# Four fixed tiles per expert with seven further tiles between them, three weight buffers and a first group in two halves, in a fused sliding-attention and mixture-of-experts kernel

## The chip, the core and the metric

The kernel runs on one core of a Trainium2 chip. The metric is the device time of one execution in microseconds (us); lower is better. All arithmetic is float32.

## What is computed

Attention with a sliding window of 128 keys and a distance bias (8 batches, 8 heads, 576 positions, head size 64), then a mixture of experts over the 4608 resulting rows of 512 numbers: each row goes to the one expert of 8 with the largest gate logit.

```python
scores = where((rel >= 0) & (rel < 128), q @ k.T / sqrt(64) - slope[h] * abs(rel), -1e9)
attn   = softmax(scores) @ v                       # (8, 8, 576, 64)
x      = attn.transpose(0, 2, 1, 3).reshape(4608, 512)
logits = x @ w_gate                                # (4608, 8)
e      = logits.argmax(1)                          # one expert per row
y      = relu(x @ w1[e]) @ w2[e]                   # w1: 512 x 1024, w2: 1024 x 512
out    = softmax(logits)[e] * y
```

The inputs are drawn with a fixed seed. Worked out from the reference, the eight experts receive 547, 614, 590, 502, 618, 462, 608 and 667 rows.

## The kernel before

**Attention.** 32 units `u` (batch `b` = u // 4, pair of heads `hp` = u % 4) run one after the other on TensorE. Unit `u` computes `scores(u)`, DVE multiplies the exponentials with the bias factors (`factors`), GpSimd adds the two halves of each window in `merge(u)` (tile `mg`, lines 439 and 442), and one unit later TensorE runs `values(u - 1)` and `totals(u - 1)`; `totals` (line 477) reads `mg`. After each batch a list of tasks (10 or 12: gate logits, picking the expert, ranking the rows, building and sending the finished rows) is worked off, up to three tasks per unit; `slow = u < 6` keeps them back at the start. A task of the last kind, `send`, issues `scatter` (line 174), an indirect DMA from GpSimd that writes 128 finished rows into the buffer `x_rows` in DRAM, each at the place that its expert and its rank within the expert give it.

**Rows that are not there.** Each expert owns 4608 rows of `x_rows`. Before any scatter, `clear_rows` (line 112) writes a marked zero row into the first `CAP` rows of each expert, one expert per unit for `u` = 1 to 8, on SyncE's DMA queue, which also carries the loads of q, k and v. The first scatter waits for all of these clears.

**Experts.** A tile is 128 rows of one expert. `NJ = 5` tiles per expert are computed whatever the routing says (`CAP` = 640 rows), so 40 tiles in 8 groups; rows past 640 are covered by further tiles of one tile each, whose expert (`xe`) and first row (`xr`) `extras` works out on DVE. `XU = 2` such tiles are always computed, after the eighth expert, and masked if empty; a loop at the end would take any more. A group goes through `gather` (SyncE DMA of its rows into `xg`, two buffers; two DMAs for a group of more than two tiles), `ready` (its weights `w1` and `w2`, 2 MB each, into one of two weight buffers), `turn` (transposes `tp`, line 734, copied to `xgT` by DVE, line 735), `layer1` (lines 744 to 751: 64 weight blocks, tile `hps`, relu into `h_sb` on DVE and ACT in turn), `tokens` (`si`, the output row numbers, lines 726 and 727, from the gathered rows) and `layer2` (line 757, tile `zp`; ACT scales it into `zo`, line 762; GpSimd scatters it to the output, line 763). The matmuls of layer 1 stream 320 columns at a time for a group of five tiles and 128 for a single tile; those of layer 2 always stream 512. In the trace each float32 matmul shows as two records.

The order of the work is that of the loop:

```python
for g, after in zip(groups, groups[1:] + [None]):
    if after is not None:
        gather(after)
        ready(after)
    layer1(g)
    tokens(g)
    if after is not None:
        turn(after)
    layer2(g)
```

SyncE issues in this order; on the other engines a scheduler may move instructions past each other, so the order per engine is shown below where it matters.

Of the kernel before, what the change touches and what calls it, by code (L numbers as in the profile page):

```python
# [15 lines left out]
P = 128  # L16
# [5 lines left out]
def kernel(  # L22
# [30 lines left out]
    NJ = 5  # L53
    CAP = NJ * P
    NX = -(-(N - CAP) // P)
    XU = 2
    NC = E * NJ + NX
    LC = NJ * HALF
# [123 lines left out]
    w_pools = [ctx.enter_context(tc.tile_pool(name="weights0", bufs=1)), None]  # L182
    n_loads = [0]

    def load_weights(w1_src, w2_src):
        w_pool = w_pools[n_loads[0] % 2]
        n_loads[0] += 1
        w1 = w_pool.tile([P, DB, F], F32, name="w1")
        w2 = w_pool.tile([P, FB, Dm], F32, name="w2")
        nc.sync.dma_start(w1[:], w1_src.rearrange("(a p) f -> p a f", p=P))  # L190
        nc.sync.dma_start(w2[:], w2_src.rearrange("(a p) d -> p a d", p=P))
        return w1, w2
# [150 lines left out]
    with tc.tile_pool(name="tab", bufs=1) as tab, \  # L343
# [233 lines left out]
        with tc.manual_schedule():  # L577
# [10 lines left out]
            for u in range(NU + 1):  # L588
                b, hp = divmod(u, HP)

                slow = u < 6
# [19 lines left out]
                do(len(tasks) if u == NU else 0 if slow else 2)  # L611
# [96 lines left out]
    def moe_pools():  # L708
        st = ExitStack()
        pools["x"] = st.enter_context(tc.tile_pool(name="moe_x", bufs=2))  # L710
        pools["wk"] = st.enter_context(tc.tile_pool(name="moe_wk", bufs=2))
        w_pools[1] = st.enter_context(tc.tile_pool(name="weights1", bufs=1))
        pools["ps"] = st.enter_context(tc.tile_pool(name="moe_ps", bufs=3, space=PSUM))
        return st
# [14 lines left out]
    def turn(g):  # L729
        g["xT"] = pools["wk"].tile([P, DB, NJ * P], F32, name="xgT")  # L730
        for j in range(g["n"]):
# [5 lines left out]
    def layer1(g):  # L737
        g["h"] = pools["wk"].tile([P, FB, NJ * P], F32, name="h_sb")
        step = min(LC, g["n"] * P)
        for fb in range(FB):  # L740
            for c in range(0, g["n"] * P, step):
                hps = pools["ps"].tile([P, LC], F32, name="hps")
                for db in range(DB):
                    nc.tensor.matmul(  # L744
                        hps[:, :step], lhsT=g["w"][0][:, db, fb * P : (fb + 1) * P],
                        rhs=g["xT"][:, db, c : c + step], start=(db == 0), stop=(db == DB - 1),
                    )
                if fb % 2 == 0:
                    nc.vector.tensor_relu(g["h"][:, fb, c : c + step], hps[:, :step])  # L749
                else:  # L750
                    nc.scalar.activation(g["h"][:, fb, c : c + step], hps[:, :step], AF.Relu)  # L751
# [26 lines left out]
    def ready(g):  # L778
        if "x" in g:
            g["w"] = fetch(g["x"])  # L780
# [4 lines left out]
    def experts(first):  # L785
        groups = [
            dict(n=NJ, e=e, rows=x_d[e * N : e * N + CAP, :], mask=masks[:, :, e, :], apart=True)
            for e in range(E)
        ]
        gather(groups[0])  # L790
        ready(groups[0])
        turn(groups[0])
        extras(first)
        for x in range(XU):
            ex = nc.sync.value_load(xe[0:1, x : x + 1], min_val=0, max_val=E - 1)
            r0 = nc.sync.value_load(xr[0:1, x : x + 1], min_val=0, max_val=E * N - P)
            groups.append(
                dict(n=1, x=ex, rows=x_d[bass.ds(r0, P), :], mask=xmasks[:, :, x : x + 1], apart=True)
            )
        for g, after in zip(groups, groups[1:] + [None]):  # L800
            if after is not None:
                gather(after)
                ready(after)
            layer1(g)
            tokens(g)
            if after is not None:
                turn(after)
            layer2(g)
# [5 lines left out]
    with tc.If(more > 0):  # L814
# [10 lines left out]
        with tc.If(nx > XU):  # L825
            with moe_pools(), tc.For_i(XU, nx, 1) as i:
# [6 lines left out]
                turn(g)  # L833
                layer1(g)
# [31 lines left out]
```

## Time and profile before

| | |
|---|---|
| median of 3 runs (lowest, highest) | 857.45 us (854.78, 859.46) |
| the profiled execution | 855.47 us, its span 853.7 us |
| TensorE busy | 802.2 us, 94% of the span |
| DVE, ACT, GpSimd busy | 227.8, 173.9, 171.5 us |
| DMA moved | 112.56 MB, mean 132 GB/s |
| mean granted TensorE clock | 0.971 of full speed |

The span runs from the first to the last instruction; the time contains it and 1.8 us around it. "Idle before" in a row is the time for which the engine stood still ahead of that work, and after the arrow stands what ended it. A weight load (PEld) runs beside the matmuls (PE). The attention part lies in the first 240 us, the experts in the rest.

### The profile page before, as it was taken

The page shows a single profiled execution, that of the slowest core. Times are in us where ns is not written, and L with a number is a line of the kernel's source. Part 1 is how long each engine was busy: PE and PEld are TensorE (multiplying, and loading weights), DVE is VectorE, ACT ScalarE, POOL GpSimd, SP SyncE. Part 2 cuts the span into 40 slices and gives each one's busy share as a digit, 9 for nine tenths or more (in the row PEclk, how much of TensorE's full clock was granted, in tenths as well). Part 3 has the DMA queues.
Part 4 walks back from the last instruction along what each step waited for, and adds up shares of the span by engine and source line. Part 5 has one row for each costly group of instructions (what it writes and reads, how often), then busy time and mean ns, then how long its engine had stood idle before and what let it go on. Part 6 is the DMA issues. An engine that isn't in the chain of part 4 may idle for free.

```text
span 853.7 us, 10090 instructions
## 1 busy us (share of the span) xinstructions
PE 802.2 (94%) x4162; PEld 511.6 (60%) x4162; DVE 227.8 (27%) x475; ACT 173.9 (20%) x410; POOL 171.5 (20%) x189
## 2 busy tenths in 40 slices
PE   4997999999679999999999999999999999999993
PEld 3775777766557547646645754764664575475481
DVE  5463777887841101101200110110120011010010
ACT  3553556545200101001001010100100110010010
POOL 5344665656500010010010001001001000100100
PEclk8898999999779999999999999999999999999997
DMA  9994895531244016017004201600701420150060
GB/s 347 342 355 191 317 336 172 193 108 52 100 160 173 19 47 246 5 45 268 1 37 164 116 25 50 232 13 37 269 0 38 171 96 25 54 190 12 37 225 5
DMA packets 47335, 112.56 MB, mean 132 GB/s; under 512 B 3503, under 2 KB 3503, under 8 KB 47280
## 3 DMA queue, kind: packets, MB, share of 16 engines
q1 hardware_dynamic: 40512, 92.89, 30.8%
q0 software_dynamic: 6240, 18.92, 5.9%
q8 instruction: 35, 0.57, 0.3%
q14 instruction: 20, 0.16, 0.1%
q10 hardware_dynamic: 528, 0.02, 0.0%
HBM read 82.37 MB, written 31.01 MB: 133 GB/s over the span
## 4 chain that ended last, share of the span: by engine, by line
issue 69%; PE 15%; POOL 9%; DVE 5%; ACT 1%; POOLq 0%; DVEq 0%
PE sp L413 5%; POOL out_dram L763 5%; PE m L458 4%; PE sm L477 2%; PE m L556 2%; POOL x_rows L174 1%; POOL mg L439 1%; DVE probs L427 1%; PE m L498 1%; POOL mg L442 1%; DVE probs L432 1%; ACT gex L536 1%; DVE lgn L532 1%; PE m L514 1%; DVE xs L559 0%
## 5 line engine op out<-in xcount | busy, mean ns | idle before, releaser
L757 PE MATMUL zp<-w,h_sb 128*128 128x512 f32 x672 | 292.4, 592 | 0.0
L744 PE MATMUL hps<-xgT,w 128*128 128x320 f32 (+1 forms) x1152 | 291.8, 415 | 0.0
L744 PEld LDWEIGHTS hps<-xgT,w 128*128 128x128 f32 x1152 | 209.0, 190 | 83.9 <-issue 4.3
L757 PEld LDWEIGHTS zp<-w,h_sb 128*128 128x128 f32 x672 | 125.8, 190 | 149.2 <-issue 149.2
L749 DVE TENSOR_SCALAR h_sb<-hps 128x320 f32<-128x320 f32 (+1 forms) x72 | 33.8, 469 | 460.6 <-PE hps L744 460.6
L763 POOL DMA_INDIRECT out_dram<-zo,si x42 | 40.8, 971 | 567.1 <-ACT zo L762 567.1
L751 ACT ACTIVATE h_sb<-hps 128x320 f32<-128x320 f32 (+1 forms) x72 | 30.2, 419 | 277.1 <-PE hps L744 277.1
L762 ACT ACTIVATE zo<-zp,xg 128x512 f32<-128x512 f32 x42 | 28.9, 687 | 279.0 <-PE zp L757 279.0
L413 PE MATMUL sp<-q_sb,k_sb 64*128 64x256 f32 (+2 forms) x640 | 71.5, 368 | 6.4 <-DMA k_sb<-in_kT_dram 6.4
L420 ACT ACTIVATE e<-sp 128x512 f32<-128x512 f32 x128 | 66.2, 599 | 48.1 <-PE sp L413 44.8
L413 PEld LDWEIGHTS sp<-q_sb,k_sb 64*128 64x128 f32 x640 | 63.0, 199 | 17.8 <-issue 11.1
L439 POOL TENSOR_TENSOR mg<-probs 128x768 f32<-128x768 f32 x31 | 57.5, 1856 | 77.8 <-DVE probs L432 29.0
L458 PE MATMUL m<-probs,v_sb 128*64 128x256 f32 (+3 forms) x768 | 64.2, 316 | 3.7 <-DVE probs L427 2.8
L458 PEld LDWEIGHTS m<-probs,v_sb 128*64 128x64 f32 x768 | 48.4, 138 | 19.9 <-DVE probs L427 2.9
L427 DVE TENSOR_TENSOR probs<-e,fac 128x1024 f32<-128x1024 f32 x32 | 43.6, 1361 | 43.8 <-ACT e L420 34.1
L174 POOL DMA_INDIRECT x_rows<-xs,slots x36 | 39.8, 1104 | 22.8 <-issue 12.0
L432 DVE TENSOR_TENSOR probs<-e,fac 128x1024 f32<-128x1024 f32 x32 | 41.9, 1309 | 0.7 <-ACT e L420 0.5
L735 DVE COPY xgT<-tp 128x512 f32<-128x512 f32 x42 | 27.7, 688 | 45.2 <-PE tp L734 45.0
L477 PE MATMUL sm<-mg,one_c 128*32 128x320 f32 (+1 forms) x256 | 24.5, 373 | 11.0 <-POOL mg L442 11.0
L734 PE MATMUL tp<-ident,xg 128*128 128x128 f32 x168 | 24.6, 289 | 10.6 <-DMA xg<-x_rows 10.5
L734 PEld LDWEIGHTS tp<-ident,xg 128*128 128x128 f32 x168 | 21.3, 150 | 20.8 <-issue 13.9
L465 ACT COPY xT<-m 128x256 f32<-128x256 f32 x64 | 25.3, 402 | 22.9 <-PE m L458 22.9
(127 smaller groups left out, 282.3 us busy)
## 6 DMA issues: line engine op xcount, KB each, us to landing
w<-in_moe_w_dram SPq DMA_DIRECT2D x20, 2048.0 KB, 11.6
x_rows<-zero_row SPq DMA_DIRECT2D x8, 1285.0 KB, 16.8
v_sb<-in_v_dram SPq DMA_DIRECT2D x8, 1024.0 KB, 7.8
q_sb<-in_qT_dram SPq DMA_DIRECT2D x7, 1152.0 KB, 7.8
k_sb<-in_kT_dram SPq DMA_DIRECT2D x7, 1152.0 KB, 11.5
xg<-x_rows SPq DMA_DIRECT2D x8, 771.0 KB, 6.0
xg<-x_rows SPq DMA_DIRECT2D x8, 514.0 KB, 3.8
v_sb<-in_v_dram SPq DMA_DIRECT2D x8, 256.0 KB, 8.1
```

What stands on the lines that cost most here:

```text
L174: ins = nc.gpsimd.indirect_dma_start(out=x_d[:, :], out_offset=bass.IndirectOffsetOnAxis(ap=slots[:, t : t + 1], axis=0), in_=row, in_offs ...
L413: nc.tensor.matmul(sps[s][par][:, c : c + n], lhsT=k_sb[b][half, hp, k_lo[j] : k_lo[j] + P], rhs=q_sb[b][half, hp, q0 : q0 + n], start=Tru ...
L420: nc.scalar.activation(exps[u][s][:, par, :], sps[s][par][:], AF.Exp, scale=D ** -0.5)
L427: nc.vector.tensor_tensor(to.rearrange("p a (j c) -> p a j c", c=2 * P), e.rearrange("p a (j c) -> p a j c", c=2 * P), fac[:, heads, None, ...
L432: nc.vector.tensor_tensor(to, e[:], fac2[:, heads, :], op=ALU.mult)
L439: eng.tensor_add(mg[:, :, : 3 * P].rearrange("p a (t c) -> p a t c", c=P), two[:, :, :, 0, :], two[:, :, :, 1, :],)
L458: nc.tensor.matmul(xp[par * HALF : (par + 1) * HALF, lo - q0 : hi - q0], lhsT=v_sb[b][:, j, h * D : (h + 1) * D], rhs=probs[u][:, par, c + ...
L477: nc.tensor.matmul(sm[g : g + 32, c : c + n], lhsT=one_c[:, hp, :], rhs=src[:, par, s0 : s0 + n], start=(hp == 0 and c == 0), stop=(hp == ...
L734: nc.tensor.transpose(tp[:, db, :], g["xg"][:, j, db * P : (db + 1) * P], ident[:])
L744: nc.tensor.matmul(hps[:, :step], lhsT=g["w"][0][:, db, fb * P : (fb + 1) * P], rhs=g["xT"][:, db, c : c + step], start=(db == 0), stop=(d ...
L757: nc.tensor.matmul(zp[:], lhsT=g["h"][:, fb, j * P : (j + 1) * P], rhs=g["w"][1][:, fb, :], start=(fb == 0), stop=(fb == FB - 1),)
L763: ins = nc.gpsimd.indirect_dma_start(out=out[:, :], out_offset=bass.IndirectOffsetOnAxis(ap=g["si"][:, j : j + 1], axis=0), in_=zo[:], in_ ...
```

## The change

It sets `NJ = 4` (so `CAP` = 512 and 32 fixed tiles) and `XU = E - 1` = 7, and puts one further tile between every two experts: 15 groups in the order 4, 1, 4, 1, ..., 4. Layer 1 now streams a whole group at once (512 columns). There are three weight buffers, and a group's weights are asked for two groups ahead. The first group goes through `turn` and `layer1` in two parts of two tiles. In attention the tasks start at u = 7 and three instead of two are taken at the end of a unit while 14 or more wait.

```diff
-    NJ = 5
+    NJ = 4
...
-    XU = 2
-    NC = E * NJ + NX
-    LC = NJ * HALF
+    XU = E - 1
+    LC = NJ * P
...
-    w_pools = [ctx.enter_context(tc.tile_pool(name="weights0", bufs=1)), None]
+    w_pools = [ctx.enter_context(tc.tile_pool(name="weights0", bufs=1)), None, None]
...
-        w_pool = w_pools[n_loads[0] % 2]
+        w_pool = w_pools[n_loads[0] % len(w_pools)]
...
-                slow = u < 6
+                slow = u < 7
...
-                do(len(tasks) if u == NU else 0 if slow else 2)
+                do(len(tasks) if u == NU else 0 if slow else 2 if len(tasks) < 14 else 3)
...
-        w_pools[1] = st.enter_context(tc.tile_pool(name="weights1", bufs=1))
+        for i in range(1, len(w_pools)):
+            w_pools[i] = st.enter_context(tc.tile_pool(name=f"weights{i}", bufs=1))
...
-    def layer1(g):
-        g["h"] = pools["wk"].tile([P, FB, NJ * P], F32, name="h_sb")
-        step = min(LC, g["n"] * P)
+    def layer1(g, tiles):
+        if tiles[0] == 0:
+            g["h"] = pools["wk"].tile([P, FB, NJ * P], F32, name="h_sb")
+        cols = slice(tiles[0] * P, (tiles[-1] + 1) * P)
+        n = len(tiles) * P
...
         if "x" in g:
-            g["w"] = fetch(g["x"])
+            x = g["x"]
+            ex = nc.sync.value_load(xe[0:1, x : x + 1], min_val=0, max_val=E - 1)
+            r0 = nc.sync.value_load(xr[0:1, x : x + 1], min_val=0, max_val=E * N - P)
+            g["rows"] = x_d[bass.ds(r0, P), :]
+            g["w"] = fetch(ex)
...
+        groups = []
+        for e in range(E):
+            groups.append(dict(n=NJ, e=e, rows=x_d[e * N : e * N + CAP, :], mask=masks[:, :, e, :], apart=True))
+            if e < XU:
+                groups.append(dict(n=1, x=e, mask=xmasks[:, :, e : e + 1], apart=True))
         gather(groups[0])
         ready(groups[0])
-        turn(groups[0])
         extras(first)
...
+        parts = [[0, 1], list(range(2, NJ))]
+        turn(groups[0], parts[0])
+        layer1(groups[0], parts[0])
+        turn(groups[0], parts[1])
+        layer1(groups[0], parts[1])
+        ready(groups[1])
+        for i, g in enumerate(groups):
+            after = groups[i + 1 : i + 3]
+            if after:
+                gather(after[0])
+            if len(after) > 1:
+                ready(after[1])
+            if i > 0:
+                layer1(g, range(g["n"]))
             tokens(g)
-            if after is not None:
-                turn(after)
+            if after:
+                turn(after[0], range(after[0]["n"]))
             layer2(g)
```

**Place 1: GpSimd in attention, around the first scatter** (`mg` is the sum of `merge`, two rows per unit; `x_rows` is the scatter). Before:

```order
L442 TENSOR_TENSOR mg<-probs 128x2x64
L550 COPY xs<-tok_i 128x2
L439 TENSOR_TENSOR mg<-probs 128x2x384
L442 TENSOR_TENSOR mg<-probs 128x2x64
L174 DMA x_rows<-xs,slots 36864x514
L550 COPY xs<-tok_i 128x2
L174 DMA x_rows<-xs,slots 36864x514 x3
L439 TENSOR_TENSOR mg<-probs 128x2x384
L442 TENSOR_TENSOR mg<-probs 128x2x64
L439 TENSOR_TENSOR mg<-probs 128x2x384
```

Now:

```order
L438 TENSOR_TENSOR mg<-probs 128x2x384
L441 TENSOR_TENSOR mg<-probs 128x2x64
L549 COPY xs<-tok_i 128x2
L173 DMA x_rows<-xs,slots 36864x514
L549 COPY xs<-tok_i 128x2
L438 TENSOR_TENSOR mg<-probs 128x2x384
L441 TENSOR_TENSOR mg<-probs 128x2x64
L173 DMA x_rows<-xs,slots 36864x514 x3
L438 TENSOR_TENSOR mg<-probs 128x2x384
L441 TENSOR_TENSOR mg<-probs 128x2x64
```

The merge of unit 9 stood behind all four scatters of the first batch; now it stands behind the first alone, and the other three follow it.

**Place 2: SyncE's queue where the experts begin** (`xg` is a gather, `w` are weights; 2838 and 2839 are the second expert's `w1` and `w2`, 2911 and 2912 those of the first further tile, 2917 and 2918 the second expert's). Before:

```order
L721 DMA xg<-x_rows 128x2x514
L721 DMA xg<-x_rows 128x3x514
L795 TENSOR_LOAD xe
L795 ISA x2
L796 TENSOR_LOAD xr
L796 ISA x2
L795 TENSOR_LOAD xe
L795 ISA x2
L796 TENSOR_LOAD xr
L796 ISA x2
L721 DMA xg<-x_rows 128x2x514
L721 DMA xg<-x_rows 128x3x514
L190 DMA w_2838<-in_moe_w_dram 128x4x1024
L191 DMA w_2839<-in_moe_w_dram 128x8x512
```

Now:

```order
L721 DMA xg<-x_rows 128x2x514 x2
L783 TENSOR_LOAD xe
L783 ISA x2
L784 TENSOR_LOAD xr
L784 ISA x2
L189 ISA
L189 DMA w_2911<-in_moe_w_dram 128x4x1024
L190 ISA
L190 DMA w_2912<-in_moe_w_dram 128x8x512
L721 ISA
L721 DMA xg<-x_rows 128x514
L189 DMA w_2917<-in_moe_w_dram 128x4x1024
```

The second gather stood ahead of the weights; now that of the first further tile stands behind 4 MB of them. From the next group on, each gather again comes ahead of the weights that are asked for with it.

**Place 3: TensorE where the experts begin** (`tp` are transposes, four per tile; `hps` is layer 1, `zp` layer 2). Before:

```order
L734 MATMUL tp<-ident,xg 128x128 x20
L744 MATMUL hps<-xgT,w_1285 128x320
L691 MATMUL tp<-n_in,ones_sq 128x1
L744 MATMUL hps<-xgT,w_1285 128x320 x63
L734 MATMUL tp<-ident,xg 128x128 x8
L757 MATMUL zp<-w_1286,h_sb 128x512
```

Now:

```order
L690 MATMUL tp<-n_in,ones_sq 128x1
L735 MATMUL tp<-ident,xg 128x128 x12
L746 MATMUL hps<-xgT,w_1285 128x256 x32
L735 MATMUL tp<-ident,xg 128x128 x8
L759 MATMUL zp<-w_1286,h_sb 128x512
L746 MATMUL hps<-xgT,w_1285 128x256 x32
L759 MATMUL zp<-w_1286,h_sb 128x512 x31
L746 MATMUL hps<-xgT,w_2911 128x128 x32
L735 MATMUL tp<-ident,xg 128x128 x8
L759 MATMUL zp<-w_2912,h_sb 128x512
```

Three tiles are now transposed ahead of the first half of layer 1; the eight transposes behind it are the fourth tile and the first further tile, which thus stands ahead of the second half. The small `n_in` matmul, on which `xe` depends, moved ahead of the transposes.

## Rows read from the trace of the kernel before

**Rows 1.** The page: busy us of each engine, share of the span, instructions.
```profile
PE 802.2 (94%) x4162; PEld 511.6 (60%) x4162; DVE 227.8 (27%) x475; ACT 173.9 (20%) x410; POOL 171.5 (20%) x189
```

**Rows 2.** Windows: busy us per engine (instructions), granted clock, DMA share, GB/s.
```profile
45.00:70.00 25.00, 24.24 (x284) 19.09 (x280) 16.71 (x33) 14.61 (x39) 7.94 (x8) 1.00 1.05 362
...
78.00:84.00 6.00, 5.22 (x26) 3.54 (x28) 2.56 (x10) 0.69 (x5) 3.01 (x5) 0.50 0.00 0
...
240.50:245.20 4.70, 4.57 (x21) 3.86 (x22) 2.96 (x6) 0.00 (x0) 0.00 (x0) 0.53 0.28 109
...
318.60:333.50 14.90, 14.90 (x57) 10.55 (x56) 2.30 (x6) 1.31 (x3) 0.00 (x0) 1.00 1.00 373
...
461.00:790.00 329.00, 329.00 (x1066) 194.75 (x1064) 34.82 (x71) 31.91 (x61) 20.41 (x21) 1.00 0.26 96
```

**Rows 3.** Timeline, SyncE: start us, us, DMA issues of two successive five-tile groups.
```profile
388.31 0.88 SPq L721 DMA_DIRECT2D xg<-x_rows  x2
...
459.29 0.88 SPq L721 DMA_DIRECT2D xg<-x_rows  x2
```

**Rows 4.** Timeline, TensorE: the first of the two single tiles.
```profile
811.46 7.31 PE L744 MATMUL hps<-xgT,w 128*128 128x128 f32 x64
818.60 0.60 PE L734 MATMUL tp<-ident,xg 128*128 128x128 f32 x4
819.04 7.03 PE L757 MATMUL zp<-w,h_sb 128*128 128x512 f32 x16
825.91 0.27 PE L744 MATMUL hps<-xgT,w 128*128 128x128 f32 x1
```

**Rows 5.** Timeline, TensorE, where the experts begin; then the last scaling and scatter.
```profile
240.56 4.76 PE L734 MATMUL tp<-ident,xg 128*128 128x128 f32 x20 [10.51 <-DMA xg<-x_rows]
245.16 0.70 PE L744 MATMUL hps<-xgT,w 128*128 128x320 f32 x2
...
840.12 0.69 ACT L762 ACTIVATE zo<-zp,xg 128x512 f32<-128x512 f32 x1 [6.59 <-PE zp L757]
841.08 0.97 POOL L763 DMA_INDIRECT out_dram<-zo,si  x1 [13.04 <-ACT zo L762]
```

**Rows 6.** Timeline of attention, TensorE and GpSimd around 70 us; who waited for the clears.
```profile
72.02 0.41 PE L477 MATMUL sm<-probs,one_c 128*32 128x128 f32 x4
78.78 1.28 PE L477 MATMUL sm<-mg,one_c 128*32 128x320 f32 x8 [6.34 <-POOL mg L442]
...
84.97 0.66 PE L556 MATMUL m<-ident,xT 128*128 128x128 f32 x4
...
70.68 1.45 POOL L174 DMA_INDIRECT x_rows<-xs,slots  x1 [7.09 <-issue]
...
76.50 1.82 POOL L439 TENSOR_TENSOR mg<-probs 128x768 f32<-128x768 f32 x1
...
  POOL x_rows L174: 7.1, 1
```

**Rows 7.** The page, DMA issues: count, KB each, us from issue to landing.
```profile
w<-in_moe_w_dram SPq DMA_DIRECT2D x20, 2048.0 KB, 11.6
x_rows<-zero_row SPq DMA_DIRECT2D x8, 1285.0 KB, 16.8
...
xg<-x_rows SPq DMA_DIRECT2D x8, 771.0 KB, 6.0
xg<-x_rows SPq DMA_DIRECT2D x8, 514.0 KB, 3.8
```

**Rows 8.** Timeline around a single tile's gather: ACT, SyncE, DVE; then `xe` at the start.
```profile
811.71 0.69 ACT L762 ACTIVATE zo<-zp,xg 128x512 f32<-128x512 f32 x1 [6.18 <-PE zp L757]
812.42 0.35 SPq L721 DMA_DIRECT2D xg<-x_rows  x1
815.57 0.16 DVE L726 TENSOR_TENSOR si<-xg,xmasks 128x1 int32<-128x1 int32 x1 [0.94 <-DMA xg<-x_rows]
...
236.70 13.75 SPq L721 DMA_DIRECT2D xg<-x_rows  x4
...
246.38 0.17 DVE L703 CAST xe<-xe_f 1x34 int32<-1x34 f32 x1
```

More of the change, by code (lines that the diff above doesn't have):

```diff
@@ L727, in tokens, with turn @@
         nc.vector.tensor_tensor(g["si"][:, :n], g["si"][:, :n], g["mask"][:, 1, :], op=ALU.bitwise_or)
-    def turn(g):
-        g["xT"] = pools["wk"].tile([P, DB, NJ * P], F32, name="xgT")
-        for j in range(g["n"]):
+    def turn(g, tiles):
+        if tiles[0] == 0:
+            g["xT"] = pools["wk"].tile([P, DB, NJ * P], F32, name="xgT")
+        for j in tiles:
             tp = pools["ps"].tile([P, DB, P], F32, name="tp", bufs=2)
@@ L735, in turn @@
             nc.vector.tensor_copy(g["xT"][:, :, j * P : (j + 1) * P], tp[:])
-    def layer1(g):
-        g["h"] = pools["wk"].tile([P, FB, NJ * P], F32, name="h_sb")
-        step = min(LC, g["n"] * P)
-        for fb in range(FB):
[L741 to L751, printed above, removed]
+    def layer1(g, tiles):
+        if tiles[0] == 0:
+            g["h"] = pools["wk"].tile([P, FB, NJ * P], F32, name="h_sb")
+        cols = slice(tiles[0] * P, (tiles[-1] + 1) * P)
+        n = len(tiles) * P
+        for fb in range(FB):
+            hps = pools["ps"].tile([P, LC], F32, name="hps")
+            for db in range(DB):
+                nc.tensor.matmul(
+                    hps[:, :n], lhsT=g["w"][0][:, db, fb * P : (fb + 1) * P], rhs=g["xT"][:, db, cols],
+                    start=(db == 0), stop=(db == DB - 1),
+                )
+            if fb % 2 == 0:
+                nc.vector.tensor_relu(g["h"][:, fb, cols], hps[:, :n])
+            else:
+                nc.scalar.activation(g["h"][:, fb, cols], hps[:, :n], AF.Relu)
     def layer2(g):
@@ L785, in experts @@
     def experts(first):
[L786 to L789, printed above, removed]
+        groups = []
[3 more added lines that the diff above has]
+                groups.append(dict(n=1, x=e, mask=xmasks[:, :, e : e + 1], apart=True))
         gather(groups[0])
         ready(groups[0])
-        turn(groups[0])
         extras(first)
[L794 to L800, printed above, removed]
-            if after is not None:
-                gather(after)
-                ready(after)
-            layer1(g)
+        parts = [[0, 1], list(range(2, NJ))]
[12 more added lines that the diff above has]
+                layer1(g, range(g["n"]))
             tokens(g)
-            if after is not None:
-                turn(after)
+            if after:
+                turn(after[0], range(after[0]["n"]))
             layer2(g)
@@ L832 @@
                 gather(g)
-                turn(g)
-                layer1(g)
+                turn(g, range(1))
+                layer1(g, range(1))
                 tokens(g)
```

## The prediction

> **What bounds the kernel now.** The page first: TensorE is busy for 802.2 of 853.7 us [rows 1]. Since a busy TensorE need not be one at full speed, the windows come next. In the experts' part it has no gap: 329.00 busy us in a stretch of 329 at full clock, with the DMA engines busy for 0.26 of it [rows 2]. There the time is the number of matmul columns, and a tile left out is a tile saved. The timeline then gives the price of a group. SyncE issues the gathers of successive five-tile groups at 388.31 and 459.29, so one group takes 70.98 us [rows 3]. The single tile at the end takes from 811.46 to 825.91, 14.45 us: 7.14 layer 1, 0.44 transposes, 6.87 layer 2 [rows 4]. Eight groups and two single tiles make 8 x 70.98 + 2 x 14.45 = 596.7 us. From the first transpose at 240.56 to the last matmul, whose result ACT takes up at 840.12, are 599.5 [rows 5]; the 2.8 above the sum lie at the start, where the granted clock is at 0.53 of full speed, the lower of its two levels (1.2 GHz), until layer 1 begins at 245.16 [rows 2, 5].
>
> Last, the gaps of TensorE before 240 us. The one that the change touches is at 72 us: `totals` waits 6.34 us for GpSimd's `mg` [rows 6]. GpSimd itself stood for 7.09 us at the first scatter, and the clears were what it waited for (the last row of rows 6). After this gap TensorE runs at the lower clock: 0.50 from 78 to 84 [rows 2].
>
> **The change, term by term.**
>
> *Tiles.* A group of four has 64 records of 512 columns in layer 1 and 64 in layer 2. Layer 2 of one tile is 16 such records in 6.87 us, 0.429 each [rows 4]; so 128 x 0.429 = 55.0, and four transposes of a tile at 0.44 add 1.8: 56.7. Pro rata from the five-tile group it is 0.8 x 70.98 = 56.8, so the two ways agree. A single tile is priced by the trace at 14.45. New sum: 8 x 56.7 + 7 x 14.45 = 554.8 against 596.7. **This term is -42.0 us.** Three tiles fewer (39 for 42) carry it; five more single tiles give back 5 x (7.14 - 6.87) = 1.4 of it, since a layer 1 of 128 columns costs 0.27 more per tile than columns alone.
>
> The narrow matmuls lose only those 0.27 us, 4% [rows 4]. The Trainium skill ("TensorE: Matmul & The Clock Gate", section "Back-to-back issue gap") gives a stream of load and matmul pairs about 81 ns per matmul at 128 columns and 131 at 512, so a column costs 2.5 times as much when narrow. An estimate by that ratio makes layer 1 of a single tile 17 us and the seven of them 69 us dearer, for a total of 875. The trace disagrees, for float32.
>
> *Fifteen weight loads for ten.* Each is 4.2 MB. The DMA engines move 373 GB/s when kept busy [rows 2], so a load is 11.3 us of transfer and fifteen are 169, beside 555 us of matmuls. A pair of groups (71.2 us) needs two loads and five tiles of rows, 26 us. Asked for two groups ahead, each load has a whole pair of groups to land. Cost 0; the cover is the four-tile group of 56.7 us.
>
> *Gathers behind single tiles.* A four-tile gather is issued when ACT has scaled the last tile of the group before, and must land during the single tile's layer 1. In the trace that order of events is: scaling at 811.71, gather issued at 812.42, layer 1 over at 818.60 [rows 8, 4]. The new gather is two pieces of 514 KB; a piece of that size lands 3.8 us after issue, and the second piece of a five-tile gather, larger, 6.0 [rows 7]. The second issue comes 0.44 us after the first (0.88 for two, [rows 3]), so: first piece at 816.2, second at 818.9 at the latest. The first transposes need the first piece alone; those of the other two tiles come 1.7 us later. Cost 0, upper end 7 x 0.3 = 2. Behind the waiting `si` on DVE [rows 8] stands one relu of the single tile, which layer 2 needs only for its seventh block.
>
> *Start of the experts.* Before, all five tiles were transposed in the slow 4.6 us. Now three tiles and the first matmuls fall into the same slow stretch, so its loss stays about 2.8 less 0.3. What is new is the single tile's transpose ahead of the second half of layer 1 (place 3). Its gather stands behind 4.2 MB of weights on SyncE (place 2). SyncE got the value `xe` only after 246.38 before, because the `n_in` matmul stood behind layer 1; now that matmul is first, so `xe` should be there by about 239, when DVE has done the routing arithmetic, and the weights go out near 241. 4.5 MB at 373 GB/s are 12 us, and a small gather has about 2.4 us of latency (3.15 from issue to use, [rows 8], less 0.7 of transfer): it lands near 255.8. The first half of layer 1 is 64 records at half of 0.429, 13.7 us, from about 243.3: it ends near 257. So the wait is 0 if `xe` is early, and up to 6 us, with 2.4 for a lowered clock, if `xe` is as late as before. I take **+1.0**, near the early end, because the order of the instructions speaks for it.
>
> The Trainium skill ("DMA: Bandwidth & Descriptors", section "HWDGE ordering") says that each DMA engine takes the descriptors of a ring in order, so the gather cannot overtake those weights. No row of this trace has a gather behind weights; without the rule the term would be 0 for certain.
>
> *Attention.* The clears shrink from five to four tiles per expert, 257 KB for each of eight, 2.1 MB in all. In that stretch the DMA engines are full at 362 GB/s (share 1.05, [rows 2]), so the last clear lands about 5.8 us earlier: the first scatter starts at 64.9 instead of 70.68. The merge that TensorE waited for now stands behind one scatter, not four (place 1): 64.9 + 1.5 for the scatter + 0.7 + 2.3 for the merge is 69.4, and `totals` wants it at 72.4. The gap of 6.34 goes, and with it the slow clock: the work from 78.78 to 84.97 is 6.2 us [rows 6] at half speed for most, of which I count 2.4 as lost. **-8.7**. The lower end is 0, if the clears land as late as before; the point is 67.9, above which the merge is late. Moving the tasks by one unit changes no TensorE work. What is late next is nothing long: the other gaps before 240 are in the first 22 us and in the wait for the last scatters, 10.51 [rows 5], which stays.
>
> *Relu, scaling, clearing of other engines*: DVE is busy for 35 of 329 us [rows 2]; nothing there becomes a bound. The tail after the last matmul is the same.
>
> **Sum.** 855.5 - 42.0 - 8.7 + 1.0 = **806 us**, against the profiled execution, which is 2.0 below the median of 857.45; the median of the new runs may lie as much above the sum.
>
> **Rivals.**
> - *The attention gap stays.* For it: the landing of the last clear is worked out from a mean rate, and the clear shares the queue with the load of the next batch. Against: the new order spares the merge three scatters in any case. Up to 8.7 comes back: 814.5. Chance 0.15.
> - *Single tiles are too short to hide the next gather.* For it: 818.9 against 818.60 has no room. Against: those seven places have no other transfer in the queue, as the weights asked for earlier have had 56 us. With 1.5 us at each of seven places, +10: 816. Chance 0.12.
> - *Slower than before: the gathers wait behind weights at all seven places.* Then each four-tile gather lands 11.3 us later, TensorE stands some 11 us and loses 2.4 more to the clock, 7 x 13.7 = 96: 902. From 7.2 us per place on it eats the 50 gained. Against: the order puts each gather ahead of the weights asked for with it (place 2). Chance 0.03.
> - *Narrow weights bind.* If each weight load of a single tile cost its full 0.19 us, layer 1 would be 64 x 0.19 = 12.2 and seven of them 35 dearer: 841. The trace has 7.14 [rows 4]. The skill's figures above point this way. Chance 0.01.
> - *The change does not do what it says*: an eighth further tile sends the kernel into the loop at its end, one unhidden load (11.3) and a tile (14.45) and its gather and branch, some 30 us: 836. The reference's counts need 1+1+1+0+1+0+1+2 = 7, and none lies within 9 rows of a boundary of 128. Chance 0.02.
> - *More is gained*: the early DMA relief removes other waits in the first 70 us. 799. Chance 0.07.
>
> **How the numbers follow.** The forecast of 806 has 0.60. The range takes in the first two rivals and the 2 us between profile and median, upward to 818, and downward the lighter clears, to 799. Left out are the slower, the narrow and the loop cases and part of the last. A measurement of this kernel can tell about 0.5%, 4.3 us, from no change. Faster by more than that: all cases but the slower one and some slack, 0.95; within: 0.02; slower: 0.03.
>
> **What would show each step.** Tiles: a fixed group and a single tile together take 71.2 us from gather to gather, without gaps of TensorE. Start: no wait of TensorE between the halves of layer 1 of more than 2 us. Attention: no gap near 72 us, first scatter near 65, first expert transpose near 232. Wrong would be: gaps of TensorE after each single tile, a clock below full in the experts' part, or a first scatter that still starts at 70.

## The result, and the profile after

| | before | the change |
|---|---|---|
| median of 4 runs each (lowest, highest) | 856.12 us (854.57, 859.46) | 809.07 us (806.76, 809.21) |
| the profiled execution, its span | 855.47, 853.7 us | 808.99, 807.3 us |
| TensorE busy | 802.2 us | 759.4 us |
| DMA moved | 112.56 MB | 130.61 MB |

The ratio is 0.9439, with a 95% interval of 0.9403 to 0.9475: 47 us less. A second measurement (the change again, in the experiments) gave 0.9441.

The page of the changed kernel, in its parts 1, 5 and 6 (busy time; groups with count, busy time and mean ns; DMA issues with us to landing):

```profile
PE 759.4 (94%) x3974; PEld 451.0 (56%) x3974; DVE 224.3 (28%) x474; ACT 169.0 (21%) x399; POOL 173.0 (21%) x186
...
L746 PE MATMUL hps<-xgT,w 128*128 128x512 f32 (+2 forms) x1024 | 272.8, 427 | 0.0
L759 PE MATMUL zp<-w,h_sb 128*128 128x512 f32 x624 | 271.6, 592 | 0.0
...
w<-in_moe_w_dram SPq DMA_DIRECT2D x30, 2048.0 KB, 13.4
x_rows<-zero_row SPq DMA_DIRECT2D x8, 1028.0 KB, 14.6
xg<-x_rows SPq DMA_DIRECT2D x16, 514.0 KB, 5.1
...
xg<-x_rows SPq DMA_DIRECT2D x7, 257.0 KB, 2.9
```

Layer 1 (`hps`) and layer 2 (`zp`, 39 x 16 = 624) have 0.0 us of idle time ahead of their groups, although the weights now take 30 issues for 20 [rows 7]. TensorE's busy share stays at 94%: the kernel is bound as it was, by fewer columns.

The experts' start on the changed kernel's timeline (TensorE, then the further tile's gather on SyncE and its first reader on DVE; columns: start us, us, engine, line, operation):

```profile
236.35 3.01 PE L735 MATMUL tp<-ident,xg 128*128 128x128 f32 x12 [5.93 <-DMA xg<-x_rows]
239.16 14.31 PE L746 MATMUL hps<-xgT,w 128*128 128x256 f32 x64
253.31 1.04 PE L735 MATMUL tp<-ident,xg 128*128 128x128 f32 x8
...
236.96 3.27 SPq L721 DMA_DIRECT2D xg<-x_rows  x1
...
252.12 0.15 DVE L726 TENSOR_TENSOR si<-xg,xmasks 128x1 int32<-128x1 int32 x1
```

The second tile pair's transposes (253.31) follow the first half of layer 1 with nothing in brackets: no wait. Then a single tile and the gather of the four-tile group behind it, two successive four-tile gathers, and the last scaling:

```profile
295.46 7.31 PE L746 MATMUL hps<-xgT,w 128*128 128x128 f32 x64
...
296.43 0.88 SPq L721 DMA_DIRECT2D xg<-x_rows  x2
...
302.02 0.16 DVE L726 TENSOR_TENSOR si<-xg,masks 128x4 int32<-128x4 int32 x1 [1.60 <-DMA xg<-x_rows]
...
302.61 1.04 PE L735 MATMUL tp<-ident,xg 128*128 128x128 f32 x8
...
367.56 0.88 SPq L721 DMA_DIRECT2D xg<-x_rows  x2
...
438.69 0.88 SPq L721 DMA_DIRECT2D xg<-x_rows  x2
...
793.86 0.69 ACT L764 ACTIVATE zo<-zp,xg 128x512 f32<-128x512 f32 x1 [6.18 <-PEq L824]
```

The rows of the gather are there at 302.02, 0.6 us before TensorE wants them at 302.61. A four-tile and a single group take 438.69 - 367.56 = 71.13 us. From the first transpose to the last scaling are 557.5 us; before, 599.6 [rows 5].

**Where the 46.5 us between the two profiled executions lie:** 42.1 in the experts, 4.2 before their first transpose (240.56 [rows 5] to 236.35), 0.2 behind them. Attention on the changed kernel's timeline, TensorE and then GpSimd and DVE, answers to rows 6:

```profile
72.59 0.48 PE L412 MATMUL sp<-q_sb,k_sb 64*128 64x256 f32 x1
...
78.53 0.73 PE L476 MATMUL sm<-mg,one_c 128*32 128x320 f32 x8 [1.08 <-POOL mg L441]
...
81.42 0.42 PE L158 MATMUL m<-pre,ones_sq 128*128 128x48 f32 x2 [1.57 <-ACT xT L464]
...
66.18 1.15 POOL L173 DMA_INDIRECT x_rows<-xs,slots  x1 [3.90 <-DVE probs L431]
...
67.49 1.82 POOL L438 TENSOR_TENSOR mg<-probs 128x768 f32<-128x768 f32 x1
69.27 1.45 POOL L441 TENSOR_TENSOR mg<-probs 128x128 f32<-128x128 f32 x1
70.88 1.79 POOL L173 DMA_INDIRECT x_rows<-xs,slots  x1 [0.16 <-issue]
72.97 0.98 POOL L173 DMA_INDIRECT x_rows<-xs,slots  x1 [0.30 <-DVE lgw L522]
74.25 0.98 POOL L173 DMA_INDIRECT x_rows<-xs,slots  x1 [0.30 <-issue]
75.24 1.84 POOL L438 TENSOR_TENSOR mg<-probs 128x768 f32<-128x768 f32 x1
77.01 1.47 POOL L441 TENSOR_TENSOR mg<-probs 128x128 f32<-128x128 f32 x1
...
75.06 3.12 DVE L426 TENSOR_TENSOR probs<-e,fac 128x1024 f32<-128x1024 f32 x1 [1.46 <-ACT e L419]
```

The first scatter starts 4.5 us earlier, the merge of unit 9 (67.49) is early enough, and the gap of 6.34 us at 72 is gone. But now three scatters (70.88, 72.97, 74.25) stand ahead of the merge of unit 10. TensorE waits 1.08 us for that merge at 78.53, and at 81.42 it waits another 1.57 us, for something else: ACT's copy `xT`, which on ACT stands behind the exponentials of the second batch's gate. The start of `scores` of some units on the timeline (us) shows what was won and lost again:

| | unit 10 | unit 11 | unit 12 | unit 13 | unit 31 | first expert transpose |
|---|---|---|---|---|---|---|
| before | 67.51 | 81.43 | 89.16 | 95.32 | 212.06 | 240.56 |
| the change | 66.34 | 72.59 | 81.99 | 90.22 | 206.84 | 236.35 |
| lead | 1.2 | 8.8 | 7.2 | 5.1 | 5.2 | 4.2 |

At unit 11 the lead is 8.8 us. Units 11 and 12 lose 3.7 of it, and 1.0 more goes at the boundary, where the last scatter took 2.23 us to issue and not 0.98 (DVE's routing arithmetic now runs beside it; that this is the reason was not tested).

The same stretch of both kernels, before and then now (columns as in rows 2):

```profile
66.00:92.00 26.00, 19.66 (x188) 14.80 (x185) 12.65 (x28) 9.88 (x29) 12.10 (x13) 0.87 0.55 206
66.00:92.00 26.00, 23.35 (x237) 17.69 (x230) 18.82 (x36) 12.10 (x34) 17.29 (x16) 0.93 0.49 167
```

TensorE stands idle for 2.65 us of it instead of 6.34, which is 3.7 won, and the granted clock is 0.93 instead of 0.87, which by my estimate is another 1.6 (0.06 of 26 us). Together that is the lead of some 5 us with which attention ends.

### The profile page after: what moved, and what is told of

Read it like the earlier page. It is cut to its first block, busy times and chain, and to the rows that moved or that the text cites. A ratio compares the mean times of both kernels' runs of the same rounds, so it can differ in the third digit from the quotient of the medians.

```text
span 807.3 us, 9802 instructions
## 1 busy us (share of the span) xinstructions
PE 759.4 (94%) x3974; PEld 451.0 (56%) x3974; DVE 224.3 (28%) x474; ACT 169.0 (21%) x399; POOL 173.0 (21%) x186
## 2 busy tenths in 40 slices
DMA packets 53606, 130.61 MB, mean 162 GB/s; under 512 B 3503, under 2 KB 3503, under 8 KB 53552
## 4 chain that ended last, share of the span: by engine, by line
issue 65%; POOL 5%; POOLq 0%; DMA 0%
POOL out_dram L765 5%; DMA x_rows<-xs,slots 0%; POOLq L765 0%; POOLq L823 0%
## 5 line engine op out<-in xcount | busy, mean ns | idle before, releaser
L746 PE MATMUL hps<-xgT,w 128*128 128x512 f32 (+2 forms) x1024 | 272.8, 427 | 0.0
L759 PE MATMUL zp<-w,h_sb 128*128 128x512 f32 x624 | 271.6, 592 | 0.0
L746 PEld LDWEIGHTS hps<-xgT,w 128*128 128x128 f32 x1024 | 160.7, 191 | 114.4 <-issue 110.9
L759 PEld LDWEIGHTS zp<-w,h_sb 128*128 128x128 f32 x624 | 116.9, 190 | 138.7 <-issue 138.7
L765 POOL DMA_INDIRECT out_dram<-zo,si x39 | 37.9, 971 | 527.7 <-ACT zo L764 527.7
L751 DVE TENSOR_SCALAR h_sb<-hps 128x128 f32<-128x128 f32 (+2 forms) x64 | 30.9, 482 | 425.3 <-PE hps L746 425.3
L753 ACT ACTIVATE h_sb<-hps 128x128 f32<-128x128 f32 (+2 forms) x64 | 27.5, 430 | 259.8 <-PE hps L746 259.8
L438 POOL TENSOR_TENSOR mg<-probs 128x768 f32<-128x768 f32 x31 | 57.5, 1856 | 72.4 <-DVE probs L431 25.5
L426 DVE TENSOR_TENSOR probs<-e,fac 128x1024 f32<-128x1024 f32 x32 | 45.9, 1435 | 43.6 <-ACT e L419 29.4
L173 POOL DMA_INDIRECT x_rows<-xs,slots x36 | 43.0, 1196 | 19.6 <-DVE cnt L170 8.2
L431 DVE TENSOR_TENSOR probs<-e,fac 128x1024 f32<-128x1024 f32 x32 | 42.1, 1316 | 0.1
L735 PEld LDWEIGHTS tp<-ident,xg 128*128 128x128 f32 x156 | 19.0, 147 | 14.1 <-DMA xg<-x_rows 6.0
```

The source lines that it names most:

```text
L173: ins = nc.gpsimd.indirect_dma_start(out=x_d[:, :], out_offset=bass.IndirectOffsetOnAxis(ap=slots[:, t : t + 1], axis=0), in_=row, in_offs ...
L426: nc.vector.tensor_tensor(to.rearrange("p a (j c) -> p a j c", c=2 * P), e.rearrange("p a (j c) -> p a j c", c=2 * P), fac[:, heads, None, ...
L431: nc.vector.tensor_tensor(to, e[:], fac2[:, heads, :], op=ALU.mult)
L438: eng.tensor_add(mg[:, :, : 3 * P].rearrange("p a (t c) -> p a t c", c=P), two[:, :, :, 0, :], two[:, :, :, 1, :],)
L735: nc.tensor.transpose(tp[:, db, :], g["xg"][:, j, db * P : (db + 1) * P], ident[:])
L746: nc.tensor.matmul(hps[:, :n], lhsT=g["w"][0][:, db, fb * P : (fb + 1) * P], rhs=g["xT"][:, db, cols], start=(db == 0), stop=(db == DB - 1),)
```

## The experiments

Each ratio is to the kernel before, run beside it on the same chip (its medians: 858.43 for the first four, 858.57 for the next four, 858.21 for the last four).

### Which part of the attention change carries what

**The old rule of tasks in the changed kernel:**

```diff
-                slow = u < 7
+                slow = u < 6
-                do(len(tasks) if u == NU else 0 if slow else 2 if len(tasks) < 14 else 3)
+                do(len(tasks) if u == NU else 0 if slow else 2)
```

> The changed kernel with the old task rule (tasks from unit 6, two at a unit's end); its clears stay small. GpSimd's order around the first scatter is then that of before: the merge of unit 9 behind four scatters. Theory (the order of merge and scatters brought the attention gain, the smaller clears only helped): first scatter near 66 us, merge done near 74, totals ready near 72, so a gap of about 2 us and a partly lowered clock there: 811 to 815 us. Rival (the smaller clears alone brought it, the task rule nothing): 807 to 810, no slower than the changed kernel's 809. If the new waits of the changed kernel near 78 to 86 us are the price of the delayed tasks, they vanish here.

Measured: 811.98 us, ratio 0.946 (0.9444 to 0.9475), first expert transpose at 239.42. The time lies in the range of the theory; the scatter comes 2 us later than it had, and the gap is longer. GpSimd's and TensorE's timeline:

```profile
68.20 1.16 POOL L173 DMA_INDIRECT x_rows<-xs,slots  x1 [4.17 <-issue]
...
74.06 1.82 POOL L438 TENSOR_TENSOR mg<-probs 128x768 f32<-128x768 f32 x1
...
76.33 1.28 PE L476 MATMUL sm<-mg,one_c 128*32 128x320 f32 x8 [3.48 <-POOL mg L441]
```

The smaller clears alone bring the first scatter to 68.20 and shorten the gap from 6.34 to 3.48 us; the merge still stands behind all four scatters.

**Clears of five tiles in the changed kernel** (zero rows are written that nothing reads):

```diff
-            x_d[e * N : e * N + CAP, :].rearrange("(j p) r -> p j r", p=P),
-            zero_row[:, None, :].to_broadcast([P, NJ, RW]),
+            x_d[e * N : e * N + CAP + P, :].rearrange("(j p) r -> p j r", p=P),
+            zero_row[:, None, :].to_broadcast([P, NJ + 1, RW]),
```

> The changed kernel, but each clear writes five tiles of zero rows again (2.1 MB more in all, nothing reads them). Theory (the last clear's landing sets the first scatter): first scatter 5 to 6 us later, near 71 to 72, merge of unit 9 done near 75, a gap of TensorE of about 3 us plus some lowered clock: 812 to 816. Rival (with one scatter ahead of the merge the clears no longer matter): 808 to 810.

Measured: 816.21 us, ratio 0.9513 (0.9496 to 0.953), first expert transpose at 241.37. That is 0.2 us above the theory's range, and its scatter (below) is about 1 us later than the theory had it.

**The kernel before with the new rule of tasks:**

```diff
-                slow = u < 6
+                slow = u < 7
-                do(len(tasks) if u == NU else 0 if slow else 2)
+                do(len(tasks) if u == NU else 0 if slow else 2 if len(tasks) < 14 else 3)
```

> The kernel before with the new task rule alone; clears and experts as before. Theory: first scatter still near 70 to 71, merge behind one scatter done near 75 instead of 78.7, so the gap of 6.3 us shrinks to about 3: 852 to 854 against 856. Rival (the gap only moves one unit on): 856 and no change.

Measured: 855.48 us, ratio 0.9968 (0.9959 to 0.9978): 3.0 us less, within the 2 to 4 of the theory. The first scatter in these two, in this order:

```profile
73.14 1.16 POOL L173 DMA_INDIRECT x_rows<-xs,slots  x1 [12.50 <-issue]
```

```profile
72.44 1.16 POOL L174 DMA_INDIRECT x_rows<-xs,slots  x1 [10.11 <-issue]
```

With the large clears the scatter comes at 72 to 73 us under the new rule of tasks, no earlier than under the old one (70.68 [rows 6]), and the rule alone is worth 0.3%. With it the clears' size is worth 0.9513 - 0.944 = 0.7% of the time, some 6 us: the clears carry most of what attention gained, and the rule pays only a little on top.

**The changed kernel without triple tasks** (the task of the seventh unit kept):

```diff
-                do(len(tasks) if u == NU else 0 if slow else 2 if len(tasks) < 14 else 3)
+                do(len(tasks) if u == NU else 0 if slow else 2)
```

> The changed kernel with tasks from unit 7, but never three at a unit's end. On GpSimd the merge of unit 9 then stands ahead of all four scatters, and that of unit 10 behind them. Theory (the waits near 78 to 86 us, some 3.5 us, come from three scatters that push the merge of unit 10 onto the same time as DVE's factors, while the second batch's gate waits): with the tasks spread out these waits shrink: 805 to 808. Rival (the same work piles up a unit later): 808 to 811.

Measured: **806.03 us, ratio 0.9401 (0.9383 to 0.9418)**, the fastest of all. Counted through the code, the triple rule takes a third task in units 8, 9 and 12 alone. The timeline without it, GpSimd, TensorE, and the first expert transpose:

```profile
66.84 0.46 POOL L441 TENSOR_TENSOR mg<-probs 128x128 f32<-128x128 f32 x1
68.37 1.90 POOL L173 DMA_INDIRECT x_rows<-xs,slots  x1 [1.08 <-issue]
...
75.95 1.47 POOL L441 TENSOR_TENSOR mg<-probs 128x128 f32<-128x128 f32 x1
...
77.48 0.73 PE L476 MATMUL sm<-mg,one_c 128*32 128x320 f32 x8 [1.36 <-POOL mg L441]
...
232.03 3.02 PE L735 MATMUL tp<-ident,xg 128*128 128x128 f32 x12 [5.85 <-DMA xg<-x_rows]
```

The merge of unit 9 is now done before the first scatter, so all four scatters run while TensorE has its sums. They all stand ahead of the merge of unit 10, and TensorE waits 1.36 us for that one, no less than in the change. What is gone is the second wait, the one for ACT. Counted through the code, the triple rule brings the last gate task of the second batch and its ranking (`place`, whose matmul is line 158) into the same unit 11; without it the ranking comes one unit behind the gate. Unit 11 starts at 71.19, unit 12 at 79.04, unit 13 at 86.94 and unit 31 at 202.13: 4.7 us ahead of the change at the end of attention, and 4.3 at the first expert transpose.

Six executions with the change's own attention code (the change, the change again, and the first four kernels of the next part) put that transpose between 235.66 and 237.68; 232.03 lies 3.6 below the lowest of them. In all six the wait at line 158 is there, with 1.4 to 1.6 us. The wait for the merge of unit 10 is not: the change again is without it, as the list of TensorE's waits from 70 to 90 us shows, whose only row is

```profile
PE m L158 <- ACT xT L464: 1.4, 1, 1.4
```

and its first expert transpose is no earlier for it (236.85). So the merge of unit 10 behind the scatters is at most a part of what costs the lead: without that wait the change again still loses 2.1 us of it in unit 12 (7.6 at units 11 and 12, 5.6 at unit 13).

Two things limit what this run shows. Its profiled execution is the fastest of its five (804.24 us), and the interval of its ratio touches that of the change again (0.9417 to 0.9464). And the kernel with three numbers changed (below), which has the same rule of tasks, has its first expert transpose at 236.78, among the six. That the rule is worth 4 us in every kernel is not shown.

### Which part of the experts' change carries what

**The first group undivided:**

```diff
-        parts = [[0, 1], list(range(2, NJ))]
-        turn(groups[0], parts[0])
-        layer1(groups[0], parts[0])
-        turn(groups[0], parts[1])
-        layer1(groups[0], parts[1])
+        turn(groups[0], range(NJ))
+        layer1(groups[0], range(NJ))
```

> The changed kernel with its first group undivided: four tiles transposed, then one layer 1 of 64 matmuls of 512 columns; the single tile's transpose goes behind it. Theory: the halves are worth little, because TensorE runs below full clock either way from 236 to about 245 and does the same columns: 807 to 811, a ratio to before of 0.942 to 0.948. Rival 1: the halves hide the second pair's scaling and copies, and without them TensorE waits 2 to 4 us more before layer 1: 811 to 814. Rival 2: the halves cost something, because their 256-column matmuls run dearer per column and the single tile's transpose is forced ahead of the second half: 803 to 806.

Measured: 811.27 us, ratio 0.9441 (0.9418 to 0.9465), the change's own ratio, as the theory has it; the time alone lies in the range of rival 1. Its layer 1 of the first group:

```profile
240.32 30.12 PE L746 MATMUL hps<-xgT,w 128*128 128x512 f32 x64 [0.78 <-DVE xgT L736]
```

From the first transpose to the last scaling this execution takes 560.4 us, against 557.5 and 558.1 in the two of the change. The 2 to 3 us lie here: a wait of 0.78 for the last copy, and a granted clock of 0.50 from 240 to 245 us, where the change has 1.00. The two kernels with a few numbers changed (below) have the group undivided too and take 558.1 and 559.2. So the halves bring nothing beyond the 2 us that these ratios can tell, and whether they bring that stays open.

**Two weight buffers, weights one group ahead:**

```diff
-    w_pools = [ctx.enter_context(tc.tile_pool(name="weights0", bufs=1)), None, None]
+    w_pools = [ctx.enter_context(tc.tile_pool(name="weights0", bufs=1)), None]
...
-        ready(groups[1])
         for i, g in enumerate(groups):
-            after = groups[i + 1 : i + 3]
+            after = groups[i + 1 : i + 2]
             if after:
+                locate(after[0])
                 gather(after[0])
-            if len(after) > 1:
-                ready(after[1])
+                ready(after[0])
```

(`locate` is the part of `ready` that reads the expert and the first row of a further tile.)

> The changed kernel with two weight buffers: weights are asked for one group ahead, behind the gather of that group. Theory: while a single tile is worked on (14.45 us) the four-tile group's rows (1.03 MB) and weights (4.2 MB) must land: 5.2 MB at 373 GB/s are 14.0 us, with 0.95 to issue and 2.4 of latency 17.4, about 3 us too long. Seven places of 3 us are 20: 829, between 822 and 840, with gaps of TensorE ahead of the four-tile groups' layer 1 and none ahead of the single tiles'. Rival: the transfers are hidden anyway (layer 1 starts on the first part of the weights), and the third buffer is worth nothing: 807 to 812.

Measured: 810.64 us, ratio 0.9437 (0.9421 to 0.9453), as the rival has it. The timeline (SyncE, then TensorE) and the window of the transfer (busy us of PE, PEld, DVE, ACT and GpSimd, granted clock, DMA share, GB/s):

```profile
370.31 0.89 SPq L721 DMA_DIRECT2D xg<-x_rows  x2
371.31 0.41 SPq L189 DMA_DIRECT2D w<-in_moe_w_dram  x1
...
376.50 1.04 PE L735 MATMUL tp<-ident,xg 128*128 128x128 f32 x8
...
385.11 7.46 PE L746 MATMUL hps<-xgT,w 128*128 128x512 f32 x17
...
371.00:384.00 13.00, 13.00 (x81) 9.84 (x80) 3.69 (x9) 1.11 (x4) 0.53 (x1) 1.00 0.99 356
```

Layer 1 begins at 385.11 without a wait, though the DMA engines were busy until just before (share 0.99). My estimate of 17.4 us had counted both weight matrices; layer 1 reads only the first, and the second is wanted 27 us later.

**The gather behind the weights:** the two blocks change places, so that in each step `ready(after[1])` comes ahead of `gather(after[0])`.

```diff
-            if after:
-                gather(after[0])
             if len(after) > 1:
                 ready(after[1])
+            if after:
+                gather(after[0])
```

> The changed kernel with the order on SyncE turned round inside each step: the weights two groups ahead first, the gather of the next group behind them. Theory (transfers of one queue land in order): behind a single tile's start the 4.2 MB take 11.3 us, the gather lands some 17.3 us after layer 2 of the group before, where the transposes want it 7.3 us after: 10 us at each of seven places and 2.4 of lowered clock, 87 in all: 896, between 870 and 905. The gathers of the single tiles have 28 us of layer 1 and stay hidden. Rival (the packets of gather and weights interleave, so the gather is late only by its share): 2 us at each place: 815 to 830. Second rival (no effect): 807 to 811.

Measured: 822.22 us, ratio 0.9581 (0.9565 to 0.9597): 12 us dearer than the change. By its time this is the first rival, by its mechanism the theory, as the rows show: SyncE and TensorE at the place that answers to 367.56 above, the waits of TensorE from 228 us on (total, times, longest), and the landing of this gather:

```profile
369.38 0.37 SPq L190 DMA_DIRECT2D w<-in_moe_w_dram  x1
370.15 1.03 SPq L721 DMA_DIRECT2D xg<-x_rows  x2
...
376.33 2.74 PE L759 MATMUL zp<-w,h_sb 128*128 128x512 f32 x6
...
380.74 1.06 PE L735 MATMUL tp<-ident,xg 128*128 128x128 f32 x8 [1.67 <-DMA xg<-x_rows]
...
PE tp L735 <- DMA xg<-x_rows: 16.1, 7, 6.4
...
xg<-x_rows SPq DMA_DIRECT2D x2, 514.0 KB, 10.9
```

Behind weights the gather takes 10.9 us to land; in the change, in the same place, 4.7. So the mechanism is there. Its size was wrong twice. Only `w2`, half of the weights, stands ahead (L190 at 369.38): the buffer of `w1` was free one layer earlier, and `w1` had gone out then. And TensorE does not stand idle for the delay, since the scheduler put six matmuls of layer 2 ahead of the transposes (376.33), leaving a wait of 1.67. Less the 6.4 us at the start, which the change has too (5.93), the waits are 9.7 us in six places. Most of the other 2 is clock: behind the longest of the six (2.44 us at 454.51) the granted clock is 0.66 from 455 to 460, by my estimate 1.7 us of matmul time lost.

**The seven single tiles after the eighth expert:**

```diff
-            if e < XU:
-                groups.append(dict(n=1, x=e, mask=xmasks[:, :, e : e + 1], apart=True))
+        for x in range(XU):
+            groups.append(dict(n=1, x=x, mask=xmasks[:, :, x : x + 1], apart=True))
```

> The changed kernel with the seven single tiles in one run behind the eighth four-tile group, with three buffers as in the change. Theory: a single tile takes 14.45 us and its weights and rows are 4.45 MB, 11.9 us at 373 GB/s, so loads asked for two groups ahead keep up, and the time is the changed kernel's: 806 to 812, a ratio of 0.942 to 0.948. Rival: seven loads in a row leave no reserve (issue, latency, output writes beside them): 1 to 3 us at each of seven places, 814 to 829, and the interleaved order is then a part of the gain.

Measured: 809.92 us, ratio 0.943 (0.9404 to 0.9455). The singles run back to back, 14.45 us each:

```profile
707.94 7.31 PE L746 MATMUL hps<-xgT,w 128*128 128x128 f32 x64
...
...
722.39 7.31 PE L746 MATMUL hps<-xgT,w 128*128 128x128 f32 x64
```

The order 4, 1, 4, 1 brings nothing either.

### The tiles alone, and one tile too few

**The change itself, again**, as the measure for the three that follow.

> The changed kernel itself, on the same chip as the three runs beside it, so that differences of 0.5% can be read. Every theory: the ratio of its first measurement, 0.944, within 0.003; 806 to 812.

Measured: 810.0 us, ratio 0.9441 (0.9417 to 0.9464).

**The kernel before with two numbers changed:**

```diff
-    NJ = 5
+    NJ = 4
-    XU = 2
+    XU = E - 1
```

> The kernel before with two numbers changed: four fixed tiles for five, seven further tiles for two (they come after the eighth expert). Two weight buffers, weights one group ahead, 256-column matmuls in layer 1, no halves, the old rule of tasks. Theory (the tiles and the smaller clears carry the whole gain; order, buffers and halves carry nothing): the time of the changed kernel with the old rule of tasks, ratio 0.946, so 809 to 815, a ratio of 0.943 to 0.949. Rival (the other parts are what makes the smaller tiles pay): each of the seven single tiles in a row waits 1 to 3 us for its weights, 819 to 833, a ratio of 0.954 to 0.970.

Measured: 811.29 us, ratio 0.946 (0.9439 to 0.9481), as expected, and the ratio of the changed kernel with the old tasks. Two numbers make the whole change but 0.2%, which lies inside the interval.

**The same with `slow = u < 7`**, so that three numbers differ from the kernel before.

> The kernel before with three numbers changed: four fixed tiles, seven further tiles, and the row tasks held back to the seventh unit, never three in a unit. Theory: the task of the seventh unit is worth what it was in the changed kernel without triple tasks (ratio 0.940 against 0.946): 803 to 809, a ratio of 0.937 to 0.943, faster than the whole change with a fifth of its lines. Rival (single tiles in a row wait, as in the run before this): 6 us below that run, 813 to 827.

Measured: 810.47 us, ratio 0.9435 (0.9416 to 0.9454): a miss, 4 us above the middle of what I expected. Its unit 31 starts at 204.13, against 202.13 in the change without triple tasks, which has the same rule; 1.4 of these 2.0 us were there at unit 3 already (29.35 against 27.96). So from unit 3 to unit 31 the two take nearly the same, 174.8 and 174.2 us, where seven executions with the change's own rule take 177.9 to 180.7. Part of that is work put off, for two more tasks are then still to be done (counted through the code). From unit 31 to the first transpose this kernel takes 32.65 us, and that one 29.90. Of the difference 1.0 is a wait of TensorE for ACT's copy `lT` (at 215.59), and 0.8 is the last scatter, which took 2.23 us to issue and not 1.44. Why the same tasks end so differently stays open.

**Six further tiles for seven**, so that the seventh goes through the loop at the end of the program:

```diff
-    XU = E - 1
+    XU = E - 2
```

> The changed kernel with six further tiles between the experts for seven: the seventh goes through the loop at the end of the program. This is the price of my rival of the eighth further tile. Theory: the loop shows what the order hides, one weight load of 11.3 us, one gather, a layer 1 and 2 that start from a lowered clock, and the branch: 16 to 25 us more than the change, 825 to 834, a ratio of 0.963 to 0.975. Rival (the tile costs nearly the same there): 2 to 6 us, 811 to 816, a ratio of 0.946 to 0.952.

Measured: 830.52 us, ratio 0.9676 (0.9656 to 0.9696), 20 us more than the change. Its last tile on TensorE:

```profile
798.89 1.09 PE L735 MATMUL tp<-ident,xg 128*128 128x128 f32 x4 [18.87 <-DVE si L726]
800.76 9.38 PE L746 MATMUL hps<-xgT,w 128*128 128x128 f32 x64 [0.78 <-DVE xgT L736]
```

18.87 us of idle time for weights and gather, and a layer 1 of 9.38 for 7.31 at a lowered clock (0.75 from 800 to 810). With the tile's own 14.45 an eighth further tile would cost some 35 us, as an estimate.

## Why the prediction was right, point by point

The prediction was 806 us, between 799 and 818; the result is 809.07. The forecast case came true, and one term of its sum came out at half its size.

- **Tiles, -42.0: right.** A four-tile and a single group take 71.13 us for the 71.2 of the sum. With the start of the experts the measured term is 557.5 - 599.6 = -42.1. The kernel with two changed numbers shows that this term needs nothing else of the change.
- **Fifteen weight loads, 0: right, and with more room than I gave it.** The cover that I named, the four-tile group and loads two groups ahead, isn't needed: with two buffers the time is the same.
- **Gathers behind single tiles, 0: right.** The rows were there 0.6 us before they were wanted; I had them 0.3 us late at worst. The rival of gathers behind weights was priced at 96 us. The run with that order shows about 12, because half of the weights go out earlier and layer 2 fills the time. Both were in the code and missed by me.
- **Start of the experts, +1.0: it was about 0.** The experts take 557.5 us in the change and 558.1 in the change again, 2.7 and 3.3 above the sum of their groups, for 2.8 before. The single tile's gather was issued at 236.96 and took 13.2 us to land, behind the weights, where such a gather takes 2.9 as a median. So it was there at 250.2, for transposes at 253.31. The Trainium skill ("DMA: Bandwidth & Descriptors", section "Queues, rings and completion order") says that each DMA engine consumes a ring's descriptors in order, though a later one may finish its write before an earlier one; the 13.2 for 2.9 here and the 10.9 for 4.7 us of the turned order agree with the order of consumption.
- **Attention, -8.7: mis-sized, it measured -4.2.** The gap at 72 us went as predicted, and the lead at unit 11 was 8.8 us. The first scatter came at 66.18 for 64.9, without harm. The step that failed is "What is late next is nothing long". I had looked at the merge of unit 9 in the new order and at nothing behind it. In units 11 and 12 TensorE now waits 1.08 us for the merge of unit 10 and 1.57 for ACT behind the second batch's gate, and the clock gave back about 1.6 us, not 2.4. The second wait is the lasting one, since it stands in every execution with the change's attention code and the first does not; by the count of the tasks, three in a unit put the gate and the ranking that needs it into one unit. Without triple tasks the first transpose comes at 232.03, where I had it ("near 232"). That the time is then 806.03, the number of the sum, is in part luck: the sum is for a profiled execution, which has 804.24 there, and the other kernel with that rule doesn't repeat the gain. What makes up the rest of it stays open. My reading that the other gaps lie in the first 22 us and in the wait for the last scatters was wrong as well: the trace of before has nine more between them, of 0.3 to 2.4 us and 9.1 together, and the change keeps them.
- **The loop rival**, an eighth further tile: priced at some 30 us, measured 20 and a tile, 35.

The error of 3 us is thus the attention term (+4.5), less the start (-1.0), and small differences between executions.

## What to carry to other kernels

When a stall is removed by moving work, follow what was moved to where it now stands, on every engine that it uses: of the 8.8 us that were won here, 3.7 were lost within two units. Of a change with many parts, try the two numbers that change the amount of work before buffers and order: where the bound engine has no gap, these have nothing to hide. A transfer's time is to be compared with the first moment at which any of it is read, part by part, and not with the load as a whole.

## What the runs showed of the hardware

DVE's product of a unit (L426) takes 1.23 us as a median, GpSimd's second sum of a merge (L441) 0.46. Where the two met, they went one after the other: in the change DVE's instruction, begun at 75.06, took 3.12 us until 78.18, while GpSimd's L438 ran its usual 1.84 until 77.08 and its L441, begun at 77.01, took 1.47 until 78.48. The three durations alone (1.84 + 1.23 + 0.46 = 3.53) fill the 3.42 us from 75.06 to 78.48. It was the same without triple tasks (1.47 at 75.95), and TensorE's wait at 78.53 ended right behind it. In the change again DVE's product began only 0.3 us before the end of GpSimd's L438; there it took 1.43, and L441 again 1.47. The Trainium skill ("SBUF — State Buffer", section "SBUF: two separate sides") states that a DVE instruction with two inputs in SBUF and a GpSimd instruction that reads SBUF exclude each other for the whole instruction, not share; the trace agrees. Which of the two goes first these rows don't settle: DVE's record begins first (75.06 against 75.24), and it was DVE that waited. A merge on GpSimd is thus to be costed with DVE's work beside it: 3.4 us here for the 2.3 that the prediction took.
